# First cells as whole 128-token blocks, eight plain float32 layer blocks and a new tile order in a fused attention, mixture-of-experts and cosine-MLP kernel

## The chip, the core and the metric

The program runs on one core of one Trainium2 chip. The metric is device time in microseconds, the median of three runs. The core has a matrix engine (TensorE, PE; its weight loads are listed apart as PEld), a vector engine (VectorE, DVE), an activation engine (ScalarE, ACT), a general engine (GpSimd, POOL) and a queue engine (SyncE, SP). Each takes its own instructions in the order in which they are written; semaphores order them against each other.

## What is computed

```python
# attention with decay: B, H, S, D = 4, 8, 768, 48
for t in range(S):
    cur = einsum('bhd,bhe->bhde', u * k[t], v[t])
    y[t] = einsum('bhd,bhde->bhe', r[t], state + cur)
    state = w * state + einsum('bhd,bhe->bhde', k[t], v[t])
x = y.transpose(0, 2, 1, 3).reshape(3072, 384)
# four experts, F = 1024, all of them for every token
p = domain_probs / domain_probs.sum(-1)
x = sum(p[:, e] * (relu(x @ w1[e]) @ w2[e]) for e in range(4))
# cosine MLP, F = 2048
h = x @ w_in
out = (h * cos(h)) @ w_out
```

All of it is float32.

## The kernel before, in words

**Layers.** The 3072 tokens are six tiles of 512 columns. A weight block holds 128 hidden units: its part of the first matrix and of the second, 128 x 768 numbers. Eight blocks (`BLK`) make a unit (one expert, or half of the cosine layer). An *item* is one block on one tile. Its up half multiplies the block by the tile in three 128-row steps (`m_up`, L570), ScalarE and VectorE apply the ReLU (`m_relu`, L584), and two items later its down half adds three 128-column results into PSUM (`m_down`, L617). Operands are pairs of float32r numbers, a high and a low part, and each product is three matmuls (high by high, high by low, low by high), so an item has 18 matmuls. Who makes the pairs: `split` (L116) for activations, `w_split` (L488) for weights, both with one copy on ScalarE and one subtraction on VectorE or GpSimd. Raw weights come through SP into three staging tiles `s` (`w_load`, L480).

**Order of the items.** `plan` lists for each unit the tiles that it visits. The first unit visits tile 0 alone, the next three visit tiles 0 and 1, then the second pass (`ps` 1) takes the other tiles. Only the very first tile visit is cut into two halves of 256 columns, so there are 16 half items and 280 whole ones.

**Attention.** It is 24 cells: a cell is one batch entry by 128 tokens, four head pairs wide. Cells 0 to 3 make tile 0, cells 4 to 7 tile 1. For each cell TensorE makes scores (16 plain float32 products of 64 x 64, `a_score_pe`, L208) and state updates (16 of 48 x 48, `a_state_pe`, L189), VectorE masks them, TensorE multiplies scores by values and queries by states. From cell 4 on (`BY_CH`) the output leaves through `a_visit` (L317), which also begins the next cell; the result goes to DRAM and is loaded back as a tile. Cells 0 to 3 instead use `a_in` and `a_out`, and `a_x` transposes their result on TensorE and splits it into `xh` and `xl`. Cells 0 and 1 and half of cell 0's tables run ahead of the first item; `l_prod` and `l_sum` make their diagonal term by matmuls. The decay tables `pw` are powers of w (`powers`, L733).

**What sets the order.** All engines' programs are written by hand in one Python loop over items (`for n in range(NI + 4)`): `mix` (L841) lays the attention steps between the matmuls of an item, `take` (L856) deals out those steps in the order of a sorted list. Ahead of the loop stands a straight sequence: loads, warm-up matmuls on dummy data (`warm`), tables, cells 0 and 1, the first weight splits. All loads go through SP.

Of the kernel before, what the change touches and what calls it, by code (L numbers as in the profile page):

```python
# [26 lines left out]
def attention_moe_cos_mlp_kernel(  # L27
# [6 lines left out]
    tok_in: bass.AP,  # L34
# [4 lines left out]
    u_rep: bass.AP,  # L39
# [73 lines left out]
    dense = [True]  # L113
    dense_ps = ps_d.tile([128, 2, 512], F32, tag="ds", name="ds_ps")
# [10 lines left out]
    def a_load_t(c, eng=None):  # L125
        b, i = cells[c]
        t = ld_p.tile([128, 2, HP, 128], F32, tag="rkt", name="rkt")
        (eng or nc.sync).dma_start(out=t, in_=rkt[b, i])
        ld.setdefault(c, {})["t"] = t

    def a_load_tok(c, eng=None):
        b, i = cells[c]
        t = ld_p.tile([128, 8, HP, D], F32, tag="tok", name="tok")
        if c >= BY_CH:
            t = t[:, 0:6]
        (eng or nc.sync).dma_start(out=t.rearrange("q x p d -> q (x p d)"), in_=(tok_ch if c >= BY_CH else tok_in)[b, i])
# [10 lines left out]
    def a_ru(c, eng=None):  # L147
        t = ld[c]["tok"][:, 0:2]
        (eng or nc.gpsimd).tensor_tensor(out=t, in0=t, in1=uu_ch if c >= BY_CH else u_tok, op=ALU.mult)

    def a_rk(c, eng=None):
        t = ld[c]["tok"]
        (eng or nc.vector).tensor_tensor(out=t[:, 0:2], in0=t[:, 0:2], in1=t[:, 2:4], op=ALU.mult)
# [6 lines left out]
    def a_kp(c, eng=None):  # L160
        t = kps[c % 2]
        (eng or nc.vector).tensor_tensor(
            out=t[:, 0:2 * HD].rearrange("q (a p d) -> q a p d", a=2, d=D),
            in0=ld[c]["tok"][:, 2:4] if c >= BY_CH else ld[c]["tok"][:, 2:7:4],
            in1=wk_ch if c >= BY_CH else wk_tok, op=ALU.mult,
        )
        ld[c]["kp"] = t

    def a_dv(c, eng=None):
        t, ds = ld[c]["tok"], ld[c]["ds"]  # L170
        if c >= BY_CH:
            return
        (eng or nc.gpsimd).tensor_tensor(
            out=t[:, 0:2], in0=t[:, 4:6], in1=ds.unsqueeze(3).to_broadcast([128, 2, HP, D]), op=ALU.mult
        )


    def at_banks(c):
        d = ld[c]
        d["ps"] = d["ps_s"] = d["ps_y"] = pair_ps  # L180
        if dense[0]:
            d["ps_s"] = dense_ps
            d["ps_y"] = ps_d.tile([128, 2, 512], F32, tag="dy", name="dy_ps")


    def cells_by(c):
        return c >= BY_CH

    def a_state_pe(c, begin):  # L189
        tok = ld[c]["tok"]  # L190
        flat = ld[c]["kp"]
        ps = ld[c]["ps_s"]
        nch = 1 if cells[c][1] == NCH - 1 else 2
        for p in range(HP):
            for ch in range(nch):
                for par in range(2):
                    a0 = 64 * (ch ^ par)

                    by = cells_by(c)
                    k0 = (ch if by else par) * HD + p * D  # L200
                    nc.tensor.matmul(
                        ps[64 * par:64 * par + D, ch, p * D:p * D + D],
                        flat[a0:a0 + 64, k0:k0 + D],
                        tok[a0:a0 + 64, 4 + (ch if by else 3 * par), p, :],
                        start=begin and p == 0, stop=True, skip_group_check=True,
                    )

    def a_score_pe(c, begin, r=None, ps=None):  # L208
        t = ld[c]["t"]
        r, ps = t[:, 0] if r is None else r, ps or ld[c]["ps"]  # L210
        for p in range(HP):
            for ch in range(2):
                for par in range(2):
                    x0, a0 = 64 * par, 64 * (ch ^ par)
                    nc.tensor.matmul(
                        ps[a0:a0 + 64, ch, HD + p * C:HD + p * C + C],
# [4 lines left out]


    def l_load(c, eng=None):
        b, i = cells[c]
        t = ld_p.tile([128, 8, HP, D], F32, tag="tok", name="tok")
        nc.sync.dma_start(out=t[:, 2:8].rearrange("q x p d -> q (x p d)"), in_=tok_in[b, i][:, 2 * HD:])
        ld.setdefault(c, {})["tok"] = t

    def l_prod(c, eng=None):
        o = prods[c % 2]  # L230
        t = ld[c]["t"]
        (eng or nc.gpsimd).tensor_tensor(out=o, in0=t[:, 0], in1=t[:, 1], op=ALU.mult)
        ld[c]["prod"] = o

    def l_sum(c):
        ps = x_bank()[:, 0:2 * HP].rearrange("q (p a) -> q p a", a=2)
        for p in range(HP):
            nc.tensor.matmul(ps[:, p, :], ld[c]["prod"][:, p, :], uw2[:, p, :], start=p == 0, stop=True, skip_group_check=True)
        ds = t_p.tile([128, 2, HP], F32, tag="dsum", name="dsum")
        nc.scalar.activation(out=ds.rearrange("q a p -> q p a"), in_=ps, func=ACTF.Copy)  # L240
        ld[c]["ds"] = ds
# [5 lines left out]
    def a_state(c):  # L247
        b, i = cells[c]
        ps = ld[c]["ps_s"]
# [7 lines left out]
    def a_seen(c):  # L257
        b, i = cells[c]
        if i < NCH - 1:
            se = t_p.tile([128, HP, D], F32, tag="se", name="se")  # L260
            nc.scalar.activation(out=se, in_=ld[c]["ps_s"][:, 1, 0:HD].rearrange("q (p d) -> q p d", d=D), func=ACTF.Copy)
            ses[c] = se
# [8 lines left out]
    def a_mask(c):  # L271
        ps = ld[c]["ps"]
        s_ = t_p.tile([128, 2, HP, C], F32, tag="s", name="s")
        nc.vector.tensor_tensor(
            out=s_.rearrange("q c p t -> q c (p t)").rearrange("q c (p t) -> q c p t", t=C),
            in0=ps[:, :, HD:HD + HP * C].rearrange("q c (p t) -> q c p t", t=C),
            in1=mask.unsqueeze(1).unsqueeze(1).to_broadcast([128, 2, HP, C]),
            op=ALU.mult,
        )
        if c >= 2:  # L280
            a_seen(c)
        if c >= BY_CH:
            nc.vector.copy_predicated(
                out=s_, mask=eye.bitcast(I32).unsqueeze(1).unsqueeze(1).to_broadcast([128, 2, HP, C]),
                data=ld[c]["ds"].unsqueeze(3).to_broadcast([128, 2, HP, C]),
            )
        ld[c]["s"] = s_

    def a_first(c):
        at_banks(c)  # L290
        a_score_pe(c, True)
        a_state_pe(c, False)
# [4 lines left out]

    def a_in(c, begin=True, stop=True):
        b, i = cells[c]
        d = ld[c]  # L300
        tok, ps, s_ = d["tok"], d["ps_y"], d["s"]
        for p in range(HP):
            for ch in range(2):
                for par in range(2):
                    x0, a0 = 64 * (ch ^ par), 64 * ch
                    nc.tensor.matmul(
                        ps[a0:a0 + 64, par, p * D:p * D + D], s_[x0:x0 + 64, ch, p, :], tok[x0:x0 + 64, 4 + 3 * par, p, :],
                        start=begin and p == 0, stop=stop and i == 0 and ch == 0, skip_group_check=True,
                    )
        if c >= ONE_GROUP or not stop:  # L310
            return
        seen = t_p.tile([128, 2, HP, 1], F32, tag="seen", name="seen")
        nc.scalar.activation(
            out=seen, in_=ps[:, :, 0:HD].rearrange("q a (p d) -> q a p d", d=D)[:, :, :, 0:1], func=ACTF.Copy
        )

    def a_visit(c):  # L317
        if c + 1 < NC_:
            at_banks(c + 1)
            a_score_pe(c + 1, True)  # L320
            a_state_pe(c + 1, False)
# [12 lines left out]
        for p in range(HP):  # L334
            for ch in range(2):
                for par in range(2):
# [11 lines left out]
        if c + 1 < NC_:  # L348
            a_mask(c + 1)
        nc.scalar.activation(out=yt[0:D, 1], in_=ps[0][0:D, 0:HP * C], func=ACTF.Copy)  # L350
        if c + 1 < NC_:
            a_state(c + 1)
            a_state2(c + 1)
        nc.vector.tensor_tensor(
            out=yt[64:64 + D], in0=ps[0][64:64 + D].rearrange("q (a t) -> q a t", a=2)[:, ::-1], in1=yt[64:64 + D], op=ALU.add
        )
# [10 lines left out]
    def a_out(c):  # L367
        if c >= BY_CH:
            if c > BY_CH:
                a_x(c - 1)  # L370
# [866 lines left out]
```

## Time and profile before

| | us |
|---|---|
| median of 3 runs | 1265.65 |
| lowest, highest | 1265.34, 1265.91 |
| time of the profiled execution | 1266.89 |
| its span, first to last instruction | 1265.1 |
| TensorE busy | 1249.9 (99%) |
| VectorE busy | 773.8 (61%) |
| ScalarE busy | 486.2 (38%) |
| GpSimd busy | 196.1 (16%) |

The profiled execution lies 1.79 us above its own span and 1.24 us above the median. TensorE's busy time counts overlapping matmuls once, and says nothing of the clock at which they ran: the granted clock stands in a column of its own in the views by stretch (1.00 is the upper of its two levels, 0.50 the lower).

### The profile page before, as it was taken

To read this page: it belongs to the slowest core of one execution; us is meant where nothing else is said; L and a number is where in the kernel's file an instruction comes from. 1 tells how busy PE (TensorE), PEld (TensorE's weight loads), DVE (VectorE), ACT (ScalarE), POOL (GpSimd) and SP (SyncE) were. 2 spreads that over 40 slices of the span, in tenths; PEclk is the share of its full clock that TensorE was granted. 3 is DMA by queue.
4 is the path that set the end of the run, shared out by engine and by line. 5 is a ranking of instruction groups with operands and counts; after the bars stand their busy time and mean duration, and the time that the engine had idled before them with its cause. 6 is when DMAs were issued, how large, how long until landed. Compare 5 with 4: busy or idle time off the path is not lost.

```text
span 1265.1 us, 20299 instructions
## 1 busy us (share of the span) xinstructions
PE 1249.9 (99%) x8346; PEld 1037.0 (82%) x8346; DVE 773.8 (61%) x1253; ACT 486.2 (38%) x859; POOL 196.1 (16%) x196
## 2 busy tenths in 40 slices
PE   7999999999999999999999999999999999999997
PEld 5988888888888888888888888888888888888886
DVE  7796757757363465546555542236777777777665
ACT  3332323224221121112211222116777777766774
POOL 6633324531000000111111111112000100010100
PEclk8999999999999999999999999999999999999999
DMA  7574434543242243123331310123001400160601
GB/s 280 175 245 149 163 114 126 171 141 98 78 143 74 69 148 106 52 93 111 123 88 54 121 55 9 59 75 125 1 1 33 167 26 25 36 198 16 197 14 41
DMA packets 70292, 126.51 MB, mean 100 GB/s; under 512 B 21457, under 2 KB 42546, under 8 KB 70194
## 3 DMA queue, kind: packets, MB, share of 16 engines
q1 hardware_dynamic: 65442, 99.87, 24.5%
q0 software_dynamic: 4608, 25.17, 6.2%
q8 instruction: 66, 1.08, 0.3%
q14 instruction: 32, 0.26, 0.1%
q10 hardware_dynamic: 144, 0.13, 0.0%
HBM read 102.29 MB, written 22.86 MB: 99 GB/s over the span
## 4 chain that ended last, share of the span: by engine, by line


## 5 line engine op out<-in xcount | busy, mean ns | idle before, releaser
L578 PE MATMUL hp<-xh,w 128*128 128x512 f32 (+1 forms) x888 | 345.2, 389 | 0.3 <-ACT xh L117 0.2
L579 PE MATMUL hp<-xl,w 128*128 128x512 f32 (+1 forms) x888 | 341.7, 385 | 0.5 <-issue 0.4
L580 PE MATMUL hp<-xh,w 128*128 128x512 f32 (+1 forms) x888 | 341.5, 385 | 0.0
L646 PE MATMUL a<-gh,w 128*128 128x512 f32 (+1 forms) x880 | 338.1, 384 | 0.0
L648 PE MATMUL a<-gl,w 128*128 128x512 f32 (+1 forms) x880 | 337.7, 384 | 0.0
L647 PE MATMUL a<-gh,w 128*128 128x512 f32 (+1 forms) x880 | 337.7, 384 | 0.0
L587 ACT ACTIVATE gh<-hp 128x512 fp32r<-128x512 f32 (+1 forms) x200 | 116.2, 581 | 550.7 <-PE hp L580 543.6
L588 DVE SCALAR_TENSOR_TENSOR gl<-hp,gh 128x512 fp32r<-128x512 f32 (+1 forms) x200 | 133.3, 668 | 302.0 <-ACT gh L587 301.3
L578 PEld LDWEIGHTS hp<-xh,w 128*128 128x128 f32 x888 | 167.7, 189 | 35.6 <-DVE gl L588 0.7
L580 PEld LDWEIGHTS hp<-xh,w 128*128 128x128 f32 x888 | 167.9, 189 | 33.7 <-issue 0.8
L579 PEld LDWEIGHTS hp<-xl,w 128*128 128x128 f32 x888 | 167.9, 189 | 32.2 <-DVE xl L118 0.3
L646 PEld LDWEIGHTS a<-gh,w 128*128 128x128 f32 x880 | 165.8, 188 | 33.1 <-DVE pm L668 0.4
L648 PEld LDWEIGHTS a<-gl,w 128*128 128x128 f32 x880 | 165.7, 188 | 32.6
L647 PEld LDWEIGHTS a<-gh,w 128*128 128x128 f32 x880 | 165.8, 188 | 32.4
L669 POOL TENSOR_TENSOR acc<-acc,pm 128x512 f32<-128x512 f32 x54 | 72.0, 1362 | 532.7 <-DVE pm L668 532.7
L607 DVE SCALAR_TENSOR_TENSOR hs<-rr,hs 128x512 f32<-128x512 f32 x96 | 67.4, 702 | 62.7 <-ACT rr L606 62.7
L599 DVE SCALAR_TENSOR_TENSOR rr<-ni,hs 128x512 f32<-128x512 int32 x96 | 66.3, 691 | 45.7 <-ACT ni L598 45.7
L605 ACT ACTIVATE rr<-rr 128x512 f32<-128x512 f32 x96 | 60.8, 633 | 86.6 <-DVE rr L600 86.6
L494 DVE TENSOR_TENSOR w<-s,w 128x768 fp32r<-128x768 f32 x60 | 66.9, 1116 | 3.6 <-ACT w L493 2.5
L496 POOL DMA_DIRECT2D w<-dec_all x32 | 17.1, 536 | 332.9 <-PE a L648 332.1
L600 DVE SCALAR_TENSOR_TENSOR rr<-ni,rr 128x512 f32<-128x512 int32 x96 | 66.5, 693 | 3.3
L118 DVE TENSOR_TENSOR gl<-hs,gh 128x512 fp32r<-128x512 f32 x96 | 66.0, 688 | 0.7 <-ACT gh L117 0.7
(137 smaller groups left out, 1006.4 us busy)
## 6 DMA issues: line engine op xcount, KB each, us to landing
s<-in_moe_wb_dram SPq DMA_DIRECT2D x64, 384.0 KB, 4.4
w<-dec_all POOLq DMA_DIRECT2D x32, 768.0 KB, 4.5
rkt<-in_rkt_dram SPq DMA_DIRECT2D x24, 512.0 KB, 6.2
draw<-in_moe_wb_dram SPq DMA_DIRECT2D x32, 384.0 KB, 4.1
dec_all<-dout SPq DMA_DIRECT2D x32, 384.0 KB, 3.1
tok<-in_tok_ch_dram SPq DMA_DIRECT2D x20, 576.0 KB, 4.3
pb<-pn SPq DMA_DIRECT2D x24, 256.0 KB, 5.1
out_dram<-acc SPq DMA_DIRECT2D x17, 256.0 KB, 2.1
```

The costliest lines, as they stand in the source:

```text
L494: (eng or nc.vector).tensor_tensor(out=t[:, 1], in0=src, in1=t[:, 0].bitcast(F32), op=ALU.subtract)
L578: nc.tensor.matmul(hp, wh[:, kk, :], x_h[:, kk, :], start=kk == 0, stop=False)
L579: nc.tensor.matmul(hp, wh[:, kk, :], x_l[:, kk, :], start=False, stop=False)
L580: nc.tensor.matmul(hp, wl[:, kk, :], x_h[:, kk, :], start=False, stop=kk == KD - 1)
L587: nc.scalar.activation(out=gh, in_=hp, func=ACTF.Relu)
L588: nc.vector.scalar_tensor_tensor(out=gl, in0=hp, scalar=0.0, in1=gh.bitcast(F32), op0=ALU.max, op1=ALU.subtract)
L600: nc.vector.scalar_tensor_tensor(out=rr, in0=ni, scalar=-PI2_LO, in1=rr, op0=ALU.mult, op1=ALU.add)
L607: nc.vector.scalar_tensor_tensor(out=hs, in0=rr, scalar=1.0, in1=hs, op0=ALU.subtract, op1=ALU.mult)
L646: nc.tensor.matmul(a, wh[:, ds], gh, start=q == 0, stop=False)
L647: nc.tensor.matmul(a, wl[:, ds], gh, start=False, stop=False)
L648: nc.tensor.matmul(a, wh[:, ds], gl, start=False, stop=q == BLK - 1)
L669: nc.gpsimd.tensor_tensor(out=o, in0=o, in1=m, op=ALU.add)
```

## The change

It does six things.

1. Cells 0 and 1 are computed as blocks of 128 tokens without states: `b_score` makes, for each head pair and side, one product of 64 x 192 and one of 64 x 128 where there were 64 x 64 products. The wide operand `rr` holds r times the decay and the same times u, so the diagonal comes out of the same products, and `l_prod`, `l_sum` and the state products of these two cells leave the sequence ahead of the loop. Their states are made inside the loop (`b_states`).
2. The first eight items (expert 0 on cells 0 and 1, 256 columns) use plain float32: unsplit weights `raw_w` and unsplit activations `x_raw`, one matmul where there were three, 6 per item.
3. Those raw weights stay in tiles that tile 1 and 2 of `x` use later; when expert 0 comes a second time, `w_split` reads them from there.
4. The first pass takes expert 0 on the low half of tile 0, expert 1 on the low and the high half, expert 0 on the high half and on tile 1, then experts 2 and 3. There are 32 half items (8 of them plain) and 272 whole ones.
5. Cells 2 and 3 use the form of the later cells; a table `ONE_AT` says at which item each cell is visited (every 4th item, then every 3rd).
6. Six of the eight raw blocks, the first three staged weights and the loads of cells 3 to 5 are issued by ScalarE.

The power table is also made with a reciprocal of 16 columns in place of 64, and the warm-up has 17 matmuls in place of 14.

```diff
+    def b_ru(c):
         for p in range(HP):
-            nc.tensor.matmul(ps[:, p, :], ld[c]["prod"][:, p, :], uw2[:, p, :], start=p == 0, stop=True, skip_group_check=True)
...
+            nc.scalar.activation(out=rr[c][:, p, :, 1], in_=rr[c][:, p, :, 0], func=ACTF.Copy, scale=uw1[:, p:p + 1])
+
+    def b_score(c, ps, ps1):
...
+        for p in range(HP):
+            wide = rr[c][:, p].rearrange("q c a t -> q (c a t)")
+            for par in range(2):
+                x = slice(64 * par, 64 * par + 64)
+                c0 = p % 2 * 3 * C
+                nc.tensor.matmul(
+                    ps[x, p // 2, c0:c0 + 3 * C], t[x, 1, p, 0:C], wide[x, 0:3 * C],
+                    start=p % 2 == 0, stop=True, skip_group_check=True,
+                )
...
+                nc.tensor.matmul(
+                    ps1[x, p * 2 * C:p * 2 * C + 2 * C], t[x, 1, p, C:2 * C], wide[x, 2 * C:4 * C],
+                    start=p == 0, stop=True, skip_group_check=True,
+                )
...
+    def b_states():
+        ps = (x_bank(), ups2[1 - item[0] % 2])
+        for c in range(N_FIRST):
+            a_state_pe(c, ps, c * HD, c == 0)
...
-    plan = [(0, 0, [(0, 0)])] + [(0, un, [(0, 0), (1, 1)]) for un in range(1, NU1)]
...
+    plan = [(0, 0, [(0, 0, low)]), (0, 1, [(0, 0, low), (0, 0, high)]), (0, 0, [(0, 0, high), (1, 1, whole)])]
+    plan += [(0, un, [(0, 0, whole), (1, 1, whole)]) for un in range(2, NU1)]
...
+        (nc.scalar if w_nl[0] < 3 else nc.sync).dma_start(out=t, in_=moe_wb[un * BLK + q])
         staged[key] = t
+
+    def raw_load(q, eng=None):
+        (eng or nc.sync).dma_start(out=raw_w[0, 0, q], in_=moe_wb[q])
...
+        if n < BLK:
+            w_raw = raw_w[ps, un, q][:, 0:DM].rearrange("p (k f) -> p k f", k=KD)
+
+            def plain(kk):
+                nc.tensor.matmul(hp, w_raw[:, kk, :], x_raw[:, kk, :], start=kk == 0, stop=kk == KD - 1)
...
+            if n < BLK:
+                nc.tensor.matmul(a, wh[:, ds], gh, start=q == 0, stop=q == BLK - 1)
...
+    ONE_AT = {c: 4 * c - 6 for c in range(N_FIRST, 9)}
+    ONE_AT.update({c: 29 + 3 * (c - 9) for c in range(9, NC_ + 1)})
...
-        warm(14)
+        warm(WARM_FIRST)
         powers()
...
+        raw_load(0)
+        a_load_tok(2)
         a_load_t(2)
...
+            if n < BLK - 2:
+                raw_load(n + 2, nc.scalar)
+            if n == 0:
+                a_load_tok(3)
+            if n == 1:
+                a_load_t(3)
+            if 2 <= n < BLK:
+                w_loads(min(BLK, w_ns[0] + 3))
+                w_splits(n - 2, nc.gpsimd if n % 2 else None)
```

TensorE where the layer items begin, before (`xh`, `xl` and `w` are split pairs, `hp` the up result; L429 transposes cell 1, L215 and L201 begin cell 2):

```order
L429 MATMUL pair_ps<-ident,yo 128x128 x3
L928 LDWEIGHTS wu_a
L928 MATMUL hp_408<-wu_b,wu_a 128x256
L928 LDWEIGHTS wu_a
L928 MATMUL hp_409<-wu_b,wu_a 128x256
L578 MATMUL hp_408<-xh_98,w 128x256
L579 MATMUL hp_408<-xl_101,w 128x256
L580 MATMUL hp_408<-xh_98,w 128x256
L215 MATMUL pair_ps<-rkt 64x64 x16
L201 MATMUL pair_ps<-tok,kp_125 48x48 x16
```

Split operands stand in the first item, and cell 2 begins inside it.

The same engine now, from the beginning of cell 2 in item 2 to item 4 (`acc_106` holds `x_raw`, `raw_xl_101` and `raw_xh_102` hold raw blocks, L659 is the plain down half):

```order
L191 MATMUL pair_ps<-rkt 64x64 x16
L177 MATMUL pair_ps<-tok,kp_127 48x48 x16
L580 MATMUL hp_342<-acc_106,raw_xl_101 128x256 x2
L659 MATMUL a_464<-gh,raw_xh_100 128x256
L659 MATMUL a_466<-gh,raw_xh_100 128x256
L659 MATMUL a_468<-gh,raw_xh_100 128x256
L580 MATMUL hp_343<-acc_106,raw_xl_101 128x256 x3
L659 MATMUL a_464<-gh,raw_xh_100 128x256
L659 MATMUL a_466<-gh,raw_xh_100 128x256
L659 MATMUL a_468<-gh,raw_xh_100 128x256
L580 MATMUL hp_342<-acc_106,raw_xh_102 128x256 x3
```

Each up half and down half is three matmuls that read a raw block, and no row ahead of them splits anything.

ScalarE behind its last work on cells 0 and 1, now (L277 writes `x_raw`, L488 loads a raw block, L137 and L128 load cells 3 to 5, L484 loads staged weights, L595 is the ReLU):

```order
L277 ACTIVATE acc_106<-ds_ps 128x3x128 x2
L787 ACTIVATE wk_ch<-px 64x384
L488 DMA raw_xl_101<-in_moe_wb_dram 128x768
L137 DMA tok<-in_tok_ch_dram 128x1152 x2
L128 DMA rkt<-in_rkt_dram 128x1024
L595 ACTIVATE gh<-hp_342 128x256
L488 DMA raw_xl_101<-in_moe_wb_dram 128x768
L128 DMA rkt<-in_rkt_dram 128x1024
L595 ACTIVATE gh<-hp_343 128x256
L488 DMA raw_xh_102<-in_moe_wb_dram 128x768
L484 DMA s<-in_moe_wb_dram 128x768 x3
L286 ACTIVATE acc_105<-hp_343 128x384
```

Before, ScalarE issued none of these loads; now the raw blocks from the third on stand behind all of its work on cells 0 and 1, with loads of later cells between them.

## Rows read from the trace of the kernel before

**Rows 1.** The page: span, and TensorE's busy line.
```profile
span 1265.1 us, 20299 instructions
PE 1249.9 (99%) x8346; PEld 1037.0 (82%) x8346; DVE 773.8 (61%) x1253; ACT 486.2 (38%) x859; POOL 196.1 (16%) x196
```

**Rows 2.** Busy time by stretch: us from:to, length, engines busy (instructions), PEclk, DMA share, GB/s.
```profile
7.36:14.74 7.38, 6.16 (x206) 5.52 (x206) 5.59 (x9) 2.20 (x9) 5.42 (x5) 1.00 1.02 409
14.74:15.91 1.17, 0.00 (x1) 0.00 (x1) 0.00 (x0) 0.00 (x0) 0.60 (x1) 0.93 1.10 367
15.91:21.08 5.17, 4.73 (x48) 3.40 (x49) 2.50 (x4) 2.05 (x5) 3.10 (x2) 0.50 0.72 278
...
25.97:27.95 1.98, 0.31 (x3) 0.10 (x2) 1.95 (x5) 0.61 (x3) 1.98 (x3) 0.99 0.82 250
...
29.43:36.88 7.45, 7.45 (x91) 6.80 (x93) 3.85 (x7) 2.73 (x5) 7.37 (x7) 0.54 0.44 154
...
70.00:80.00 10.00, 9.36 (x173) 8.01 (x172) 9.87 (x15) 4.56 (x10) 4.50 (x4) 1.00 0.75 222
...
400.00:600.00 200.00, 200.00 (x884) 165.62 (x883) 109.84 (x212) 38.88 (x62) 11.48 (x9) 1.00 0.30 95
```

**Rows 3.** Timeline of TensorE: start us, us, operation, tile, shape, count.
```profile
1.35 5.23 PE L704 MATMUL hp<-wu_b,wu_a 128*128 128x512 bf16 x14 [1.35 <-DVE wu_b L869]
...
10.24 1.05 PE L238 MATMUL px<-uw,acc 128*128 128x2 f32 x8
...
21.08 0.58 PE L578 MATMUL hp<-xh,w 128*128 128x256 f32 x1 [0.15 <-ACT xh L117]
...
32.19 0.41 PE L578 MATMUL hp<-xh,w 128*128 128x256 f32 x1
32.41 0.41 PE L579 MATMUL hp<-xl,w 128*128 128x256 f32 x1
...
39.49 0.68 PE L306 MATMUL pair_ps<-tok,s 64*64 64x48 f32 x32
...
48.70 0.28 PE L578 MATMUL hp<-xh,w 128*128 128x256 f32 x1
...
50.86 0.28 PE L578 MATMUL hp<-xh,w 128*128 128x256 f32 x1
...
55.63 0.69 PE L215 MATMUL pair_ps<-rkt 64*64 64x64 f32 x32
56.14 0.54 PE L201 MATMUL pair_ps<-tok,kp 64*48 64x48 f32 x32
56.50 0.23 PE L330 MATMUL px<-s,tok 64*48 64x64 f32 x2
...
56.95 0.22 PE L339 MATMUL px<-rkt,st 48*48 48x64 f32 x2
...
57.35 0.22 PE L339 MATMUL hp<-rkt,st 48*48 48x64 f32 x2
...
66.63 0.69 PE L215 MATMUL pair_ps<-rkt 64*64 64x64 f32 x32
```

**Rows 4.** Timeline of VectorE ahead of the first item.
```profile
2.86 1.39 DVE L748 TENSOR_TENSOR pw<-pw 128x4 f32<-128x4 f32 x6
4.28 1.75 DVE L750 RECIPROCAL pw<-pw 128x256 f32<-128x256 f32 x1
...
6.37 0.68 DVE L141 TENSOR_TENSOR rkt<-rkt,pw 128x512 f32<-128x512 f32 x1
```

**Rows 5.** Timeline of ScalarE ahead of the first item.
```profile
19.04 0.49 ACT L117 ACTIVATE xh<-px 128x384 fp32r<-128x384 f32 x1 [1.15 <-PE px L429]
```

**Rows 6.** Loads of staged weights at line 485, 19 to 27 us: from issue to landing.
```profile
DMA to landing us min/median/max: 2.9/2.9/4.0
```

**Rows 7.** Waits, 60 to 1200 us: who waited for what, us, times, longest.
```profile
ACT xh L117 <- DMA acc<-yd: 5.7, 1, 5.7
```

More of the change, by code (lines that the diff above doesn't have):

```diff
@@ L186, in cells_by, with a_state_pe @@
[L186 to L193, printed above, removed]
+    def a_state_pe(c, ps, c0, begin):
+        tok, flat = ld[c]["tok"], ld[c]["kp"]
         for p in range(HP):
[L195 removed]
+            for ch in range(1 if cells[c][1] == NCH - 1 else 2):
                 for par in range(2):
[L197 to L200 removed]
+                    a0, k0 = 64 * (ch ^ par), ch * HD + p * D
@@ new lines, in b_off, with b_mask, wide @@
+    def b_off(c):
+        so = part_of(2 * c, HP * 4 * C, HP * C).rearrange("q (p t) -> q p t", t=C)
+        nc.scalar.activation(out=so.rearrange("q (b p) t -> q b p t", b=2), in_=ld[c]["first"][:, :, :, 2], func=ACTF.Copy)
+        ld[c]["so"] = so
+    def b_mask(c):
+        d = ld[c]
+        s_ = t_p.tile([128, 2, HP, C], F32, tag="s", name="s")
+        d["s"] = s_
+        parts = (
+            (s_[:, 0].rearrange("q (b p) t -> q b p t", b=2), d["first"], [128, 2, 2, C]),
+            (s_[:, 1], d["second"], [128, HP, C]),
+        )
+        def wide(x, shape):
+            for _ in shape[2:]:
+                x = x.unsqueeze(1)
+            return x.to_broadcast(shape)
+        for to, ps, shape in parts:
+            nc.vector.tensor_tensor(out=to, in0=ps[:, :, 0] if ps is d["second"] else ps[:, :, :, 0], in1=wide(mask, shape), op=ALU.mult)
+        for to, ps, shape in parts:
+            nc.vector.copy_predicated(out=to, mask=wide(eye.bitcast(I32), shape), data=ps[:, :, 1] if ps is d["second"] else ps[:, :, :, 1])
@@ new lines, in b_in @@
+    def b_in(c, ps):
+        d = ld[c]
+        tok, s_, so = d["tok"], d["s"], d["so"]
+        d["ps_y"] = ps
+        for p in range(HP):
+            for par in range(2):
+                x = slice(64 * par, 64 * par + 64)
+                for a0, with_, v_ in ((0, s_[x, 0, p, :], 4), (64, s_[x, 1, p, :], 3), (64, so[x, p, :], 4)):
+                    nc.tensor.matmul(
+                        ps[a0:a0 + 64, par, p * D:p * D + D], with_, tok[x, v_, p, :],
+                        start=p == 0 and with_ is not so and (a0 == 0 or v_ == 3), stop=v_ == 4, skip_group_check=True,
+                    )
@@ L295, in a_first @@
         a_state2(c)
[L298 to L315, printed above, removed]
     def a_visit(c):
         if c + 1 < NC_:
-            at_banks(c + 1)
-            a_score_pe(c + 1, True)
-            a_state_pe(c + 1, False)
+            a_begin_pe(c + 1)
         b, i = cells[c]
@@ L392, in a_out @@
[L392 to L404 removed]
+        if c > N_FIRST:
+            a_x(c - 1)
@@ L559, in attention_moe_cos_mlp_kernel @@
     for ps, un, tiles_ in plan:
-        for i, j in tiles_:
-            for a, b in ([(0, 2), (2, 4)] if not items else [(0, 4)]):
-                items += [(ps, un, j, q, a, b, i) for q in range(BLK)]
+        for i, j, (a, b) in tiles_:
+            items += [(ps, un, j, q, a, b, i) for q in range(BLK)]
     gts = {}
@@ L730, in setup @@
             )
+        nc.gpsimd.tensor_tensor(out=eye, in0=ident[:, 0:64], in1=ident[:, 64:128], op=ALU.add)
     def powers():
@@ L818, in lag @@
         return 3 if items[n][1] >= NU1 or (ahead < NI and items[ahead][1] >= NU1) else 2
-    N_UNIT = [next(n for n in range(NI) if items[n][0:2] == x) for x in units] + [NI]
+    N_UNIT = [next(n for n in range(BLK, NI) if items[n][0:2] == x) for x in units] + [NI]
     def w_ahead(n, g):
@@ new lines, in attention_moe_cos_mlp_kernel @@
+        b_score(0, pair_ps, x_bank())
+        b_off(0)
+        tails()
+        b_mask(0)
+        b_score(1, dense_ps[0], ps_d.tile([128, TB], F32, tag="up", name="up"))
+        b_off(1)
+        b_mask(1)
+        a_ru(2)
+        a_kt(2)
+        b_in(0, dense_ps[1][:, :, 0:HD])
+        b_y(0)
+        pt = table()
+        table2(pt, 0)
+        b_in(1, pair_ps[:, :, 0:HD])
+        b_y(1)
+        b_x(0, dense_ps[0][:, 0])
+        b_x(1, dense_ps[0][:, 1])
+        table2(pt, 1)
+        a_r(2)
@@ L924, in attention_moe_cos_mlp_kernel @@
+        a_rk(2)
+        a_sum(2)
+        for c in range(N_FIRST + 1):
+            a_kp(c)
         ps_d_ctx.close()
```

481 lines of the change are left out of this document (208 added, 273 removed).

## The prediction

> **What bounds the kernel now.** I read the page first. TensorE is busy in 1249.9 of 1265.1 us [rows 1]: whatever the change does must show as TensorE work, as time in which it waits, or as its clock. Then the table by stretch. From 400 to 600 us, 884 matmuls of 512 columns start one every 0.226 us at the full clock [rows 2]; nothing can be gained there, and the change leaves that part alone. The first 51 us are the other kind. TensorE does no matmul from 14.74 to 15.91 us; the clock then stands at 0.50 until 25.97, a second pause follows with 0.31 us of work in 1.98, and from 29.43 to 36.88 the clock is down again [rows 2]. The first layer matmul starts at 21.08 us, and item 8, the ninth, at 50.86 [rows 3]. So I compare the two kernels at the start of item 8, and then add what is left over differently.
>
> **The chain ahead of the first item.** VectorE makes the power table from 2.9 to 6.0 us [rows 4]. Now four of the six doublings remain (0.9 us), the reciprocal has 64 elements a partition in place of 256 (0.5 in place of 1.75), and four doublings of 16 and 32 columns are added (0.25 to 0.3 each): done at 5.4. Four products of 512 elements at 0.6 apart [rows 4] end at 7.8. ScalarE's eight small copies run beside them to about 8.1. The warm-up, 14 matmuls in 5.2 us [rows 3], becomes 17; three more of 512 columns add 0.7 [rows 2], so it ends at 7.2, about when the first scores can begin.
>
> The unknown price is a **plain float32 matmul with many columns**. The trace records each as two. Lower bound: two passes like a float32r one of 256 columns, 0.12 each (18 matmuls from 48.70 to 50.86) [rows 3], so 0.24 us. Upper bound: two passes of 512 columns, 0.45 [rows 2], plus two weight loads that nothing hides, 0.13 each by L238, whose moving operand has only two columns [rows 3]: 0.71. The nearest rows are small plain products with equal weights and other column counts: 32 records of 48 columns take 0.36 us (56.14 to 56.50) and 32 of 64 columns 0.45 (56.50 to 56.95) [rows 3], with four quadrants working side by side. So 16 columns cost 0.011 us a record and quadrant, 0.7 ns a column; one pass at full clock costs 0.12/256, under 0.5. That lies nearer to two cycles a column in each record. I take 0.45 and keep both ends.
>
> The Trainium skill (Perfetto Trace Analysis, Engine Utilization) halves the array's rate for FP32_LOW_HIGH; read as the rate of a whole product rather than of each record, a plain product of 256 columns would take as long as one pass of 512. The slope above speaks against that reading, but it is a rival below.
>
> At 0.45 per 256 columns, a cell's wide scores (4 pairs x 320 columns, two sides side by side) take 2.3 us: TensorE ends them at 9.5 and 11.7. Then a chain across engines: copy and mask of cell 1 to 13.5, 48 records of `b_in` 1.0 (0.68 for 32 [rows 3]), copy 0.5, transposes 0.5, copy 0.5 [rows 5]. The first plain matmul can start at **16.0**, 5.1 us sooner than now. TensorE pauses here, but for no more than half a microsecond.
>
> **Items 0 to 7.** An up or a down half is now 3 x 0.45 = 1.35 us. Items 0 and 1 end at 18.7. From item 2 on the raw blocks come through ScalarE, which issues the first one only after its last copy, at 16.3. A load of this size lands 2.9 us after issue when the queue is empty [rows 6]: 19.2, a wait of 0.5. Item 2 takes 1.35 up, 1.35 down, and the states and the begin of cell 2: two sets of state products 0.72, scores and states 0.87 (55.63 to 56.50 [rows 3]); it ends at 23.5. Behind the third raw block, ScalarE issues two `tok` and an `rkt` before the next raw one. With 409 GB/s when the engines are full [rows 2], 2.5 MB to the end of the fourth block need 6.1 us after a first microsecond, plus 0.7 to land: 24.1, a wait of 0.6. Items 3 and 4 end at 29.5. The sixth raw block stands behind 5.6 MB (another `rkt`, three staged weights, another `tok`): 31.6, a wait of **2.1**. Items 5 to 7 take 8.1, with 1.6 for the visit of cell 2 and the begin of cell 3. Item 8 begins at **41.3**, 9.6 us sooner than now. The x and w splits that stood between cells and item 0 are then beside TensorE; their cover is these items, and without it each pair costs what ScalarE and VectorE need.
>
> **What is left behind item 8.** Two plain down halves instead of two of nine matmuls: +0.5. Eight whole items are cut in halves: 16 x 2.16 [rows 3] - 8 x 18 x 0.226 [rows 2] = +2.0. One more visit and one more begin of a cell: 0.93 - 0.24 and 0.87 [rows 3] = +1.6. The tile halves that are loaded back from DRAM stand on ScalarE with a lag of two half items; a wait of 5.7 us for such a load is there before as well [rows 7] and cost TensorE nothing visible, but half items give it less cover: +0.5, bounded by 0 and 3. The rest has the same products, weights and tail: 0.
>
> Sum: -9.6 + 0.5 + 2.0 + 1.6 + 0.5 = **-5.0 us** against the profiled execution, whose span is 1265.1 and own time 1266.89; the same on the median of 1265.65 gives **1260.6**. About 0.2%, or 2.5 us, is what a measurement of this kernel can tell from no change.
>
> **Rivals.** *The clock falls after the wait for the sixth block.* Before, 1.7 us without work was followed by 7.45 us at the lower level [rows 2], where matmuls are 0.21 apart and not 0.12 (32.19 to 32.41) [rows 3]. The same here loses 3.3 us: 1263.9, no change to speak of. For it: the pause is of that size. Against: loads that come 1 us sooner, or a lower clock already in items 0 to 2, which would swallow the wait, remove it.
>
> *VectorE bounds the half-width stretch.* Cells still come about 11 us apart there (55.63 to 66.63 [rows 3]), with two ReLU remainders in place of one. From 70 to 80 us VectorE was busy 9.87 of 10 and TensorE lost 0.64 [rows 2]; over some 62 us of half items and cells that is 4.0 in place of the 0.5 above, and the result 1264.1. Against: unit 0 and unit 1 stay on TensorE longer, so fewer weights are split per microsecond.
>
> *Plain products are cheap.* At 0.24 the scores end 2.1 us sooner, and with them ScalarE's loads; then items 5 to 7 follow the loads, item 8 begins at 35.3, and the sum is -12.2: 1253.5. For it: the lower bound is a real row, and the slope of 0.7 ns lies between the two cases. Against: it lies nearer to the dear one. The Trainium skill's rate (Perfetto Trace Analysis, Engine Utilization), read for the whole product, would be this case.
>
> *The lower clock holds through the whole plain stretch* and the change is slower. Place: from the last scores to item 8. Price: 2 us in the chain, then 18.9 us of plain products and 3.2 of cells at 1.7 to 1.8 times their length, without the waits: item 8 at about 57, +10.7, 1276. It decides from some 24 us at the lower level on; before, 17 of the 21 us from 15.91 to 36.88 were like that [rows 2]. Against: the chain has no pause of 1.2 us like the one at 14.74, and items 0 and 1 are dense.
>
> *The early start is not there*: the chain ahead of item 0 is as long as before because the wide scores need 0.71 per product; then plain items also cost 11 us more, less 3.2 of waits, and the time is about 1268.
>
> **How the numbers follow.** Forecast case 0.46 (1257 to 1263), clock after the wait 0.22, VectorE 0.10, cheap products 0.09, clock throughout 0.08, no early start 0.05. Faster by over 0.2%: nearly all of the first, a third of the clock case, the cheap one, a little of VectorE's: 0.64. Within 0.2%: 0.23. Slower: 0.13. The range 1253.5 to 1268 takes in the bounds of the plain price and leaves out the clock throughout and the outer parts of the others.
>
> **What would show it.** Right: first plain matmul near 16 us, plain products 0.45 apart, item 8 near 41, a pause of TensorE before item 5 whose releaser is a raw load, and the same 0.226 per matmul after 110 us. Wrong: a clock of 0.50 for more than 10 us after 16; plain products at 0.25 or 0.7; TensorE waiting for VectorE between 45 and 105 us; item 8 later than 47.

## The result, and the profile after

The changed kernel takes 1273.89 us (median of 6 runs, 1272.25 to 1274.27) against 1265.66 us of the kernel before, run beside it: a ratio of 1.0062, interval 1.0049 to 1.0075. It is 8.2 us slower. The forecast was 1260.6 and faster; the range ended at 1268.

The page of the changed kernel, span, busy times, and one DMA queue that will matter (packets, MB, share):

```profile
span 1272.1 us, 20442 instructions
...
PE 1251.3 (98%) x8421; PEld 1041.2 (82%) x8421; DVE 775.6 (61%) x1268; ACT 492.3 (39%) x879; POOL 183.8 (14%) x185
...
q8 instruction: 67, 1.10, 0.4%
```

Against [rows 1] the span grew by 7.0 us, and TensorE's busy time only by 1.4. So 5.6 us are idle time, and the first question is where TensorE stands still. Busy time by stretch answers it (columns as in [rows 2]):

```profile
15.00:17.54 2.54, 1.33 (x11) 0.89 (x9) 1.03 (x3) 1.72 (x4) 0.00 (x0) 1.00 0.00 0
17.54:24.88 7.34, 7.34 (x154) 5.96 (x152) 2.94 (x6) 1.50 (x4) 1.22 (x2) 1.00 0.98 358
24.88:26.75 1.87, 0.00 (x2) 0.03 (x1) 1.31 (x2) 0.83 (x3) 1.52 (x4) 1.00 0.99 394
26.75:32.17 5.42, 5.42 (x24) 4.45 (x24) 1.10 (x2) 2.29 (x5) 3.44 (x3) 1.00 1.03 409
32.17:34.36 2.19, 0.00 (x0) 0.03 (x1) 2.19 (x2) 1.17 (x3) 2.19 (x3) 1.00 1.06 397
34.36:39.05 4.69, 4.69 (x107) 3.90 (x108) 4.59 (x9) 0.98 (x2) 1.87 (x1) 1.00 0.68 268
...
105.80:107.80 2.00, 0.00 (x1) 0.00 (x0) 2.00 (x5) 0.00 (x0) 0.27 (x1) 1.00 0.94 302
107.80:110.00 2.20, 2.20 (x87) 2.07 (x91) 0.47 (x2) 0.00 (x0) 0.00 (x0) 0.74 0.94 360
110.00:112.00 2.00, 2.00 (x59) 1.85 (x52) 1.24 (x2) 0.49 (x1) 0.00 (x0) 0.50 0.92 368
112.00:114.00 2.00, 2.00 (x17) 2.00 (x17) 1.57 (x3) 1.49 (x5) 1.12 (x2) 0.93 0.25 71
...
400.00:600.00 200.00, 200.00 (x884) 165.62 (x883) 106.54 (x206) 37.41 (x60) 11.48 (x9) 1.00 0.30 93
```

The last row is that of [rows 2] again, 884 matmuls: the long rest did not change. The half clock that filled most of 15.91 to 36.88 before is gone. In its place stand pauses of 1.87 and 2.19 us in the plain stretch, and one of 2.00 at 105.80 in which VectorE is busy all the time and behind which the clock falls.

TensorE's timeline at these places (in brackets the idle time ahead and who ended it):

```profile
15.02 0.33 PE L276 MATMUL ds_ps<-ident,yo 128*128 128x128 f32 x1
16.20 0.55 PE L276 MATMUL ds_ps<-ident,yo 128*128 128x128 f32 x3 [0.63 <-ACT acc L277]
17.32 0.38 PE L937 MATMUL hp<-wu_b,wu_a 128*128 128x256 bf16 x2 [0.58 <-ACT acc L277]
17.54 0.38 PE L580 MATMUL hp<-acc,raw_xh 128*128 128x256 f32 x1
...
26.75 0.45 PE L580 MATMUL hp<-acc,raw_xl 128*128 128x256 f32 x1 [1.87 <-DMA raw_xl<-in_moe_wb_dram]
...
34.36 0.45 PE L580 MATMUL hp<-acc,raw_xh 128*128 128x256 f32 x1 [2.20 <-DMA raw_xh<-in_moe_wb_dram]
...
40.24 0.21 PE L359 MATMUL px<-s,tok 64*48 64x64 f32 x1 [1.19 <-issue]
...
45.60 0.47 PE L586 MATMUL hp<-xh,w 128*128 128x256 f32 x1
...
60.98 0.39 PE L586 MATMUL hp<-xh,w 128*128 128x256 f32 x1 [1.57 <-DVE gl L600]
...
107.80 0.39 PE L586 MATMUL hp<-xh,w 128*128 128x256 f32 x1 [2.00 <-DVE gl L600]
```

Three kinds of wait: for raw blocks (26.75, 34.36), for nothing that the trace shows (40.24, in the middle of a run of equal products), and for `gl`, the ReLU remainder on VectorE (60.98, 107.80).

Item 8 starts at 45.60, 5.3 us sooner than in [rows 3]. From there I compare equal remaining work. The half items end with item 31; item 32 starts at 117.99 (first matmul of the item in the timeline), and items 8 to 31 take 72.4 us. Item 24 before starts at 111.08, but there the down halves of two whole items are still to come, here those of two half items. Two items later these are done, and what is left is the same. First the changed kernel, then the kernel before:

```profile
126.38 0.40 PE L586 MATMUL hp<-xh,w 128*128 128x512 f32 x1
```

```profile
121.36 0.39 PE L578 MATMUL hp<-xh,w 128*128 128x512 f32 x1
```

So the 5.3 us ahead have become 5.0 behind: 80.8 us from item 8 on instead of 70.5, a loss of 10.3. From item 86 to the end the distance is 7.5. Most of the loss lies between 45 and 118 us.

VectorE's timeline ahead of the wait at 60.98:

```profile
56.53 0.41 DVE L600 SCALAR_TENSOR_TENSOR gl<-hp,gh 128x256 fp32r<-128x256 f32 x1
56.87 1.02 DVE L496 TENSOR_TENSOR w<-s,w 128x768 fp32r<-128x768 f32 x1
57.81 0.86 DVE L157 TENSOR_TENSOR tok<-tok 128x384 f32<-128x384 f32 x1
58.59 1.54 DVE L166 TENSOR_TENSOR kp<-tok,wk_ch 128x384 f32<-128x384 f32 x1
60.06 0.54 DVE L161 TENSOR_REDUCE dsum<-tok 128x8 f32<-128x384 f32 x1
60.52 0.74 DVE L600 SCALAR_TENSOR_TENSOR gl<-hp,gh 128x256 fp32r<-128x256 f32 x2
```

ScalarE at the same time, the two copies that these two remainders read:

```profile
56.57 0.37 ACT L599 ACTIVATE gh<-hp 128x256 fp32r<-128x256 f32 x1
58.37 0.38 ACT L599 ACTIVATE gh<-hp 128x256 fp32r<-128x256 f32 x1 [1.43 <-PE hp L588]
```

`gh` of item 11 is there at 56.94. Its `gl` could run then, but it stands in line behind a weight split and three operations for the next cell, and runs at 60.52, 3.6 us later. A half item lasts 2.16 us, and item 13 writes the up buffer that `gl` of item 11 still has to read.

### The profile page after: what moved, and what is told of

Same layout as the page of the kernel before. It is cut to its first block, busy times and chain, and to the rows that moved or that the text cites. A ratio compares the mean times of both kernels' runs of the same rounds, so it can differ in the third digit from the quotient of the medians.

```text
span 1272.1 us, 20442 instructions
## 1 busy us (share of the span) xinstructions
PE 1251.3 (98%) x8421; PEld 1041.2 (82%) x8421; DVE 775.6 (61%) x1268; ACT 492.3 (39%) x879; POOL 183.8 (14%) x185
## 4 chain that ended last, share of the span: by engine, by line
## 5 line engine op out<-in xcount | busy, mean ns | idle before, releaser
L586 PE MATMUL hp<-xh,w 128*128 128x512 f32 (+1 forms) x888 | 341.8, 385 | 4.2 <-DVE gl L600 4.0
L587 PE MATMUL hp<-xl,w 128*128 128x512 f32 (+1 forms) x888 | 338.3, 381 | 0.6 <-DVE xl L118 0.5
L588 PE MATMUL hp<-xh,w 128*128 128x512 f32 (+1 forms) x888 | 338.0, 381 | 0.0
L684 POOL TENSOR_TENSOR acc<-acc,pm 128x512 f32<-128x512 f32 (+1 forms) x57 | 72.5, 1300 | 550.4 <-DVE pm L683 550.4
L117 ACT ACTIVATE gh<-hs 128x512 fp32r<-128x512 f32 x96 | 60.7, 633 | 8.6 <-DVE hs L619 8.5
```

Of the source, the lines that this page charges most:

```text
L586: nc.tensor.matmul(hp, wh[:, kk, :], x_h[:, kk, :], start=kk == 0, stop=False)
L587: nc.tensor.matmul(hp, wh[:, kk, :], x_l[:, kk, :], start=False, stop=False)
L588: nc.tensor.matmul(hp, wl[:, kk, :], x_h[:, kk, :], start=False, stop=kk == KD - 1)
L684: nc.gpsimd.tensor_tensor(out=o, in0=o, in1=m, op=ALU.add)
```

## The experiments

Each time below is a median, and "less" is less than the changed kernel's 1273.89. The kernel before, run beside each, gave 1266.4 to 1266.6 instead of 1265.66, so such a difference is good to about 1 us; the ratio is the firmer number.

**Theories.** *VectorE's line*: bursts of cell work stand ahead of `gl` in VectorE's order. *Loads*: ScalarE issues them late. Rivals: the DMA rate sets the landing whoever issues; VectorE has too much work, whatever the order; a gain at one place is eaten at the next.

### Loads by SyncE, less work on VectorE, and both

```diff
-        (nc.scalar if N_FIRST < c < 6 else nc.sync).dma_start(out=t, in_=rkt[b, i])
+        nc.sync.dma_start(out=t, in_=rkt[b, i])
...
-        (nc.scalar if w_nl[0] < 3 else nc.sync).dma_start(out=t, in_=moe_wb[un * BLK + q])
+        nc.sync.dma_start(out=t, in_=moe_wb[un * BLK + q])
...
-                raw_load(n + 2, nc.scalar)
+                raw_load(n + 2)
```

> The changed kernel with all its loads issued by SyncE again (six raw blocks, the first three staged weights, tok and rkt of cells 3 to 5). If ScalarE's place in line makes the raw blocks late: the waits of 1.87 and 2.20 us before 26.75 and 34.36 us fall below 0.5 each, item 8 starts near 41.5 us instead of 45.60, and the time falls by 3 to 4 us, to about 1270. If the DMA engines' rate sets the landing and not the issuer: both waits stay within 0.5 us and the time stays at 1273 to 1275. If VectorE bounds items 8 to 31: item 8 starts sooner, but the pauses behind it grow by as much, and the time stays within 1 us of 1273.9.

1270.50 us, ratio to before 1.0037 (1.0025 to 1.0050): 3.4 us less. TensorE's waits from 17 to 45 us are now all that follow; no raw block is among them:

```profile
PE px L359 <- issue: 1.2, 1, 1.2
PE hp L937 <- ACT acc L277: 0.6, 1, 0.6
PE a L659 <- issue: 0.6, 1, 0.6
```

Item 8 starts at 41.60, and item 32 3.85 us sooner than in the changed kernel: next to nothing of the gain is lost behind it. The order of issue had made the blocks late, not the DMA engines' rate (their share is 1.03 from 20 to 24 us here too).

```diff
     def a_rk(c):
+        if 3 <= c <= 9:
+            return
...
-        nc.vector.tensor_reduce(out=ds, in_=ld[c]["tok"][:, 0:2], axis=AX.X, op=ALU.add)
+        if not 3 <= c <= 9:
+            nc.vector.tensor_reduce(out=ds, in_=ld[c]["tok"][:, 0:2], axis=AX.X, op=ALU.add)
...
-        nc.vector.copy_predicated(
+        if not 3 <= c <= 9:
+            nc.vector.copy_predicated(
```

> The changed kernel without three VectorE operations of cells 3 to 9: the product of tok with itself, its row sum, and the copy of that sum onto the diagonal of the scores (the output lacks the diagonal term of these cells). If VectorE's queue makes TensorE wait between items 8 and 31: the 8.2 us that are lost there fall to 3 or less, the pauses whose releaser is the ReLU remainder on VectorE vanish, and the time is about 1268.5. If these pauses come from loads or from ScalarE: no change before 117 us over 1 us, 1273 to 1275. Item 8 starts within 0.5 us of 45.60 in both cases.

1269.41 us, 1.0023 (1.0014 to 1.0032), 4.5 less. The wait for `gl` between 45 and 118 us falls from 3.6 to 0.5 us, and items 8 to 31 take 67.8 us instead of 72.4.

> The two edits together: all loads by SyncE, and the three VectorE operations of cells 3 to 9 left out. If late raw blocks and VectorE's queue are two separate losses, their gains add: about 1265 (9 us less). If a sooner item 8 only meets VectorE's queue sooner, the load edit gains more here, beside the lighter VectorE, than alone. If neither is the cause: 1273 to 1275.

1266.28 us, 1.0001 (0.9992 to 1.0010), 7.6 less; item 80 starts 7.5 us sooner, against 3.9 and 4.1 for the edits alone. Two separate losses, and within the noise they add.

### Weight splits on GpSimd, alone and with the loads

```diff
-                w_splits(BLK * (g + 1) + w_ahead(n, g))
+                w_splits(BLK * (g + 1) + w_ahead(n, g), nc.gpsimd if n < 32 else None)
```

> The changed kernel with the subtraction of the weight splits of items 8 to 31 on GpSimd instead of VectorE. If it is VectorE's count of work there that makes TensorE wait: the 8.2 us fall by 3 to 5, 1269 to 1271. If VectorE's operations grow while GpSimd works (0.55 us against 1.36 to 1.54 were seen): VectorE's busy time from 45 to 118 us falls by less than half of what the splits took, and the time is between 1273 and 1276. If VectorE is not the cause: no change.

1268.99 us, 1.0020 (1.0011 to 1.0029), 4.9 less, and no wait for `gl` from 45 to 118 us. Of the second expectation the part on VectorE held as well, its time (1273 to 1276) did not. First the changed kernel (busy time 45 to 118 us, then VectorE's groups by shape: busy us, mean ns), then this one:

```profile
45.00:118.00 73.00, 68.79 (x1184) 65.70 (x1183) 59.79 (x96) 25.84 (x60) 31.53 (x30) 0.98 0.55 166
...
L166 DVE TENSOR_TENSOR kp<-tok,wk_ch 128x384 f32<-128x384 f32 x6 | 5.3, 877 | 0.0
L496 DVE TENSOR_TENSOR w<-raw_xh,w 128x768 fp32r<-128x768 f32 x4 | 5.1, 1272 | 0.3 <-ACT w L495 0.3
```

```profile
45.00:118.00 73.00, 71.46 (x1324) 67.98 (x1323) 54.51 (x94) 27.14 (x63) 51.03 (x42) 1.00 0.56 170
...
L166 DVE TENSOR_TENSOR kp<-tok,wk_ch 128x384 f32<-128x384 f32 x7 | 8.8, 1250 | 0.0
```

Some 14 us of splits left VectorE (eleven, 0.9 to 2.0 us each), but its busy time fell by 5.3 only, with one more cell in the window: beside a busier GpSimd one `kp` takes 1.25 us instead of 0.88. VectorE's busy share only fell from 0.82 to 0.75, and the pauses went. That speaks for what stands ahead of `gl`, and not for VectorE's sum of work in this stretch; the reordering below tries it alone.

> All loads by SyncE, and the weight splits of items 8 to 31 on GpSimd: the two edits that gained 3.9 and 4.8 us in the starts of item 80, now together. If late loads and VectorE's queue are separate losses, the gains add: item 80 starts 8 to 9 us sooner than in the changed kernel, and the time is 1265.0 to 1266.5, level with the kernel before. If the sooner start only meets GpSimd's or VectorE's queue: 1268 to 1270.

1265.28 us, 0.9995 (0.9985 to 1.0005): level with the kernel before. Item 80 starts 8.4 us sooner, against 3.9 + 4.8.

### More up buffers, or another order

```diff
-        hp = ups2[n % 2][:, 0:(b - a) * 128]
+        h0 = 256 * (n // 2 % 2) if b - a == 2 else 0
+        hp = ups2[n % 2][:, h0:h0 + (b - a) * 128]
```

> The changed kernel with four up buffers instead of two for the half items (a half item fills half of a bank, so the items n and n+2 take the two halves); no instruction is moved to another engine and none is left out. If TensorE waits because two half items give VectorE only some 2 us to read the up result (the pauses of 1.57 and 2.00 us before 60.98 and 107.80, and the low clock behind the second): these pauses vanish, the time falls by 4 to 6 us, to 1268 to 1270. If VectorE simply has too much work in this stretch: the pauses come two items later at another wait (the down products wait for the ReLU remainder), and the time falls by less than 2 us.

1273.64 us, 1.0058 (1.0045 to 1.0071): no gain. Both pauses stand where they stood, 1.56 and 2.00 us, and still at `gl`. Item 13 now writes the first half of the bank, `gl` of item 11 reads the second half, and TensorE waits for it all the same. So the edit did not take the wait away and tells nothing on the number of buffers.

> All loads by SyncE and four up buffers for the half items, the weight splits on VectorE as in the changed kernel. If two buffers of half items are what makes VectorE's bursts cost time: 8 to 10 us less than the changed kernel, 1264 to 1266. If VectorE has too much work: 1268 to 1270.

1271.22 us, 1.0038 (1.0026 to 1.0051), as with the loads alone, for the same reason.

The theory can be tried with no change of work or buffers, by the order on VectorE alone:

```diff
+            behind = [x for x in extra if BLK <= n < 32 and x[0] in (a_rk, a_kp, a_sum)]
+            extra = [x for x in extra if x not in behind]
...
             mix(main, extra)
+            for g_, c_ in behind:
+                g_(c_)
```

> The changed kernel with the same instructions on the same engines; only VectorE's order changes: in items 8 to 31 the product of tok, kp and the row sum of the next cell stand behind the ReLU remainder of their item instead of ahead of it (seven places). If it is the place in VectorE's line that costs time: the pauses of 1.57 and 2.00 us before 60.98 and 107.80, and the low clock behind the second, go, and item 32 starts 4 to 5.5 us sooner than 117.99; the time is 1268.5 to 1270. If VectorE simply has too much to do there: the pauses move to the next item or to the begin of the cell (which needs kp), and the time stays above 1272.

1270.57 us, 1.0040 (1.0027 to 1.0054), 3.3 less. VectorE's timeline at the same place as above:

```profile
56.74 0.42 DVE L600 SCALAR_TENSOR_TENSOR gl<-hp,gh 128x256 fp32r<-128x256 f32 x1
57.07 1.03 DVE L496 TENSOR_TENSOR w<-s,w 128x768 fp32r<-128x768 f32 x1
58.02 0.41 DVE L600 SCALAR_TENSOR_TENSOR gl<-hp,gh 128x256 fp32r<-128x256 f32 x1
58.36 0.54 DVE L157 TENSOR_TENSOR tok<-tok 128x384 f32<-128x384 f32 x1
58.83 1.54 DVE L166 TENSOR_TENSOR kp<-tok,wk_ch 128x384 f32<-128x384 f32 x1
60.29 0.54 DVE L161 TENSOR_REDUCE dsum<-tok 128x8 f32<-128x384 f32 x1
```

TensorE's waits from 45 to 118 us there:

```profile
PE pair_ps L177 <- DVE kp L166: 1.1, 2, 0.9
PE hp L587 <- DVE xl L118: 0.5, 1, 0.5
PE hp L586 <- DVE gl L600: 0.2, 1, 0.2
```

`gl` runs at 58.02 instead of 60.52; both pauses and the low clock behind the second are gone (1.00 in each stretch from 102 to 112 us). Items 8 to 31 take 67.7 us, as without the three operations. Of these 4.7 us, 1.2 come back in item 32: `kp`, now later, makes the begin of a cell wait. Same instructions, same engines, so the place in line is shown as the cause of the two pauses and of the low clock behind the second.

The lag of each `gl` behind its `gh` in the traces agrees. In items 8 to 31 of the changed kernel it was 3.6 and 4.6 us at the two pauses and at most 2.5 elsewhere. With the new order it was at most 2.5, and in the kernel before, from 50 to 115 us, at most 2.3; there no wait for `gl` is over 0.4 us.

### A pause that waits for nothing

```diff
-            nc.tensor.matmul(hp, wu_a, wu_b, start=True, stop=True)
+            for x in (0, 256):
+                nc.tensor.matmul(hp[:, x:x + 256], wu_a, wu_b[:, x:x + 256], start=True, stop=True)
```

> The kernel with all loads by SyncE, with 34 warm-up matmuls of 256 columns in place of 17 of 512: TensorE's work is the same, but every later instruction stands 34 records further back. If the pause of 1.16 us in the middle of cell 2's visit (record 961 of TensorE, with no releaser, in every run so far) comes from the fetch of TensorE's own instructions in blocks of 256: the pause is again ahead of record 961, which is then a product some 8 matmuls earlier in the visit, 1.0 to 2.5 us long, and others may come or go at records 961 plus a multiple of 256; the time is 1269.5 to 1271.5. If it comes from data (a state, a score or a token tile): the pause stays ahead of the same product, record 995.

1268.47 us, 1.0016 (1.0007 to 1.0025), 2.0 less than with the loads alone and below the range expected. In the traces 1.7 of it lie in items 8 to 31 (70.8 us for 72.5): the same pause of 2.00 us stands there, but the clock behind it stayed at 1.00. The pause at record 961 went; one of the same kind came ahead of record 705 = 961 - 256, in the begin of cell 2 (timeline):

```profile
21.23 0.55 PE L177 MATMUL pair_ps<-tok,kp 64*48 64x48 f32 x30
23.58 0.20 PE L177 MATMUL pair_ps<-tok,kp 64*48 64x48 f32 x1 [1.80 <-issue]
```

It follows the count of TensorE's instructions and not the data. "In every run so far" is too much: the pause at 961 was not there where the three operations were left out alone, nor with four up halves alone, nor with the new order alone. In these three the clock was at 0.50 just before (see below), and TensorE came to record 961 later, 2.7 to 3.2 us after the start of the packet that is described next. But every pause of over 0.4 us with no releaser ("issue"), in the 13 traces from the changed kernel on, from 17 to 130 us, stands ahead of record 705, 961 or 1729: steps of 256 and 3 x 256. The 0.6 ahead of L659 in the first experiment's waits is 705. Queue q8 above moves packets of 16 KB, 67 in the whole execution, and TensorE's 16,966 records make 66.3 blocks of 256. All these pauses ended 2.3 to 2.7 us after the start of such a packet.

### Faster versions

Five edits on top of the loads by SyncE: splits on GpSimd, four up halves, and three small ones:

```diff
-            if n == 5:
+            if n == 6:
                 prob_norm()
...
+    ONE_AT[19] = 60
...
-        b_x(1, dense_ps[0][:, 1])
+        b_x(1, dense_ps[1][:, 1])
```

> A try at a faster kernel: loads by SyncE, splits of items 8 to 31 on GpSimd, four up buffers for half items, the normalising of the probabilities one item later (item 6 waited 1.2 us for VectorE), cell 19 visited one item later (item 59 lost 1.2 us there), and the transposes of cell 1 into a bank of their own (TensorE waited 0.63 us for ScalarE's copy of cell 0). If these pauses are all separate: 11 to 12 us less than the changed kernel, 1262 to 1263. If they only move on to the next wait: 1265 to 1267.

1264.42 us, 0.9984 (0.9973 to 0.9996), 9.5 less than the changed kernel. Item 59 no longer waits, and the first plain product starts at 16.09. But the pause at record 961 grew to 2.34 us, and one of its kind, 1.12 us, came at 1729. The 11 to 12 us expected were not reached.

> Loads by SyncE and the new order on VectorE together (splits on VectorE, two up buffers), with three small edits: probabilities normalised one item later, cell 19 visited one item later, the transposes of cell 1 in another bank. If the losses are separate: 3.9 for the loads, 4 to 5 for the order, 1.2 for cell 19 and 0.5 for the bank: 1262.5 to 1264.5, faster than the kernel before. If the order only moves the pauses: 1267 to 1269.

1267.16 us, 1.0004 (0.9994 to 1.0014). The profiled execution took 1264.58, the twelve runs 1263.22 to 1269.66. Why they spread so is open: only one of them was profiled.

The last one takes the edits of the first of these two without the four up halves (and not the new order), and shares the loads between the two engines:

```diff
-            if n < BLK - 2:
-                raw_load(n + 2, nc.scalar)
+            if n < BLK - 3:
+                raw_load(n + 2)
+            if n == 4:
+                raw_load(7)
...
-        (nc.scalar if N_FIRST < c < 6 else nc.sync).dma_start(out=t, in_=rkt[b, i])
+        (nc.scalar if c in (4, 5) else nc.sync).dma_start(out=t, in_=rkt[b, i])
```

> The try at a faster kernel of before (splits of items 8 to 31 on GpSimd, the three small edits, two up buffers again), with another sharing of the loads: SyncE issues the raw blocks and the loads of cell 3 at once, ScalarE at its own pace the first three staged weights and the loads of cells 4 and 5. The pause of 2.34 us ahead of TensorE's record 961 was there with all loads on SyncE. If TensorE's code block waits behind loads that were issued long before they are needed: its packet starts sooner than 34 us, the pause falls below 1 us, the raw blocks are still in time, and the time is 1260.5 to 1262.5. If the pause does not depend on the loads ahead of it: it stays at 2.0 to 2.6 us, and the time is 1263.5 to 1265.5. If ScalarE's share makes raw blocks or staged weights late again: new waits before items 3 to 7, 1265 or more.

**1263.20 us, 0.9977 (0.9966 to 0.9987)**: faster than both kernels, by 3.2 us than the one before and by 10.7 than the changed one. TensorE crosses record 705 at 25.3 us; the packet for the block from 961 on starts at 29.2. With all loads on SyncE and the same other edits (and four up halves) it started at 34.2, though 705 was crossed at 25.4. The pause at 961 is gone. In its place TensorE waits for VectorE in item 6 (17 to 45 us):

```profile
PE pair_ps L177 <- DVE kp L166: 1.7, 1, 1.7
PE a L659 <- issue: 0.6, 1, 0.6
```

A pause of 1.24 us at record 1729 is in its trace as well. Which of the two kept it from 1262.5 was not tried.

## Why the prediction was wrong

**Ahead of item 0: 1.5 us too early.** The scores were right (7.61 to 9.83 us: 2.2 per cell for 2.3 forecast), and so was the plain product: items 0 and 1 have 1.30 us per half, 0.433 per 256 columns for 0.45. The rival of cheap products fell. The step that failed is "transposes 0.5, copy 0.5": counted once, for one cell. There are two cells in series, 1.18 us apart (15.02, 16.20), since both write one PSUM tile that ScalarE's copy still reads. With the second cell in another tile TensorE's wait of 0.63 went. That is 0.6 of the 1.5 us. Another 0.6 stand ahead of it: the copy of cell 1's result starts at 15.13 for 14.5. The last 0.3 lie between the last copy and the first product.

**Items 0 to 7: 4.3 us late at item 8** (45.60 for 41.3), the 1.5 included. The waits for raw blocks were 0, 1.87 and 2.20 us for 0.5, 0.6 and 2.1: 0.9 more. The pause at record 961, 1.2 us, was in no term. The rest, 0.7, was not followed further.

**The clock.** In this trace neither rival that rested on it came: 1.00 in all plain stretches, even behind pauses of 1.87 and 2.19 us. It fell where I had not forecast it, at 107.80. For the rival after the sixth block's wait this was luck. Three more traces have the same plain stretch and the same wait (2.0 to 2.2 us): without the three operations, with four up halves, with the new order. Behind it their clock was at 0.50 until 38 to 39 us, and item 5 took 3.9, 4.1 and 4.4 us instead of 2.7. With the new order:

```profile
34.00:36.00 2.00, 1.60 (x4) 1.33 (x5) 2.00 (x2) 0.00 (x0) 2.00 (x2) 0.65 1.02 401
36.00:38.00 2.00, 2.00 (x6) 1.58 (x5) 1.97 (x5) 0.38 (x1) 0.26 (x1) 0.50 0.81 311
```

So that mechanism was right, at a price of 1.3 to 1.7 us for 3.3 forecast, and it did not make the time wrong here.

**Behind item 8: the step that decided.** The terms gave +0.5 + 2.0 + 1.6 + 0.5 = 4.6 us; the stretch to equal remaining work grew by 10.3. "Eight whole items are cut in halves: +2.0" counted matmuls and took half items to cost nothing else. Of the missing 5.7 us the two waits for `gl` are 3.6. The low clock behind the second is some 1.2, an estimate: with four up halves both waits were the same but the clock stayed at 1.00, and the stretch took 79.6 us for 80.8. The last 0.9 is open. This was my rival of VectorE, whose sign ("TensorE waiting for VectorE between 45 and 105 us") came as written; but it had a chance of 0.10 and a price of 4.0 us, taken from a busy share and spread over the stretch. The loss does not follow the share: it comes in lumps, where the run of operations in VectorE's line ahead of `gl` exceeds the time until the up buffer is needed. That this time is half as long for half items is my reading; the edit meant to try it, four up halves, did not take the wait away. After item 34 another 2.5 came, where I had put 0: 1.8 about item 59 (waits of 0.9 for `kp` and 0.4 for `gl`) and 0.7 in items 84 and 85.

Together 4.3 + 5.7 + 2.5 = 12.5 us on the forecast -5.0 make +7.5, of 8.2 measured.

## What to carry to other kernels

When a step is cut in halves, other engines should have less time to answer: look in the answering engine's own order for the longest run ahead of the answer and compare that, not its busy share, with the new time. Put the answer that TensorE waits for ahead of work that is only due later; here that gained 4.7 us and gave 1.2 back, since the work that moved was soon due itself. Loads that are wanted first should not be issued behind an engine's own work. That loads wanted late should not be queued far ahead fits the last experiment, but is not shown alone.

## What was unexpected in the hardware

**TensorE's own instructions can be late.** In the changed kernel TensorE crossed record 705 at 27.9 us, and the 16 KB packet that belongs to record 961 on started at 37.8, while the DMA engines were full (share 0.98 to 1.06 from 17.54 to 34.36 us). Behind it, up to 90 us, seven packets started 0.1 to 1.9 us behind a crossing (the share was 0.55 from 45 to 118 us). A cell's small products use 256 records in some 2.3 us (1473 to 1729), so a late block shows as a pause of 0.5 to 2.3 us. The Trainium skill (Runtime: NRT & Kernel Launch, Instruction fetch mechanics) has instructions refilled in blocks of 256, which the spacing here confirms, and calls the cost mostly hidden, which these pauses do not bear out. That the packet waits behind loads already queued fits the last experiment (29.2 instead of 34.2 us), but is not shown by itself.

The kernel before has such a pause too, in the middle of 32 equal products:

```profile
15.91 0.89 PE L306 MATMUL dy_ps<-tok,s 64*64 64x48 f32 x22 [1.17 <-issue]
```

It stands ahead of record 449 = 705 - 256 and ended 2.3 us after the start of a 16 KB packet (13.58). It is the pause at 14.74 that the prediction took for a matter of the chain, and the 0.50 of the first layer items came behind it. In the changed kernel TensorE comes to record 449 at 20.9 us, without a pause. How much of the early gain comes from this no run here separates.

**A pause and the clock.** 2.00 us without work at 105.80, among float32r half items, were followed by a granted clock of 0.74, 0.50 and 0.93. With all loads by SyncE the same pause was again followed by 0.50. With four up halves, alone and with these loads, and with the warm-up matmuls cut in halves, it was followed by 1.00. The wait of 2.0 to 2.2 us among plain float32 products was followed by 1.00 in two traces and by 0.50 in three. So neither the length of the pause nor the kind of product decides, and what does no run here tells. A low stretch cost some 1.2 to 1.7 us. Each kernel was profiled once, so two traces can differ by that much for this reason alone.
